# A recurrence and a long convolution on one core: a fourth spectrum buffer, a fourth input pair, fewer and larger evictions, and a new hand-written order

## The chip, the cores and the metric

One core of a Trainium2 chip runs the whole kernel in one launch. The metric is the device time of that launch in microseconds; the median of three runs is given, and lower is better.

## The reference

Two layers follow one another, for 4 batches, 6272 time steps and 256 channels. The first is a gated recurrence along time, the second a gate with a circular convolution over the full sequence, done in the reference by FFT. Cut to what matters:

```python
sig = 1.0 / (1.0 + np.exp(-f_logit))
f = lower_bound + (1.0 - lower_bound) * sig
h = np.zeros((B, D))
for t in range(S):
    h = f[:, t] * h + (1.0 - f[:, t]) * x[:, t]
    a[:, t] = h                                  # a: input of the second layer

x1, x2, x3 = split(a @ w_proj, 3)                # 256 channels each
X2 = np.fft.rfft(x2, n=S, axis=1)
H = np.fft.rfft(filter_fft, n=S, axis=0)
y = x1 * np.fft.irfft(X2 * H, n=S, axis=1) * x3
out = y @ w_out
```

## The kernel before

**How the work is tiled.** The sequence length is 6272 = 128 x 49, and the transforms are done as matmuls with small tables, in two steps each. A filter transform at the start makes the spectrum H of all channels in 16 units (`NU`), which is written to device memory and read back, unit by unit, in every batch.

**The start (`prepare`).** 13 groups of the filter, four of the 49 rows each and the last of one row, are loaded (line 610) into raw buffers that later serve other tiles. Each group is cast into one of two staging buffers `afs` (kind `fr`, line 616; the instruction carries a helper's line, 281 on ACT, 286 on DVE, 293 on POOL), rotated by matmuls in fp32r (`rot`, line 621) and evicted from PSUM in two halves, one into each of the tiles `f2` (kind `f2`, line 625). When all are there, the first filter transform (`FF1`, line 646) and the second (`FF2`, line 664) run over the 16 units, with evictions `afs` and `hw` between them, and pairs of units are stored to device memory (`hst`, line 673). `warm` (line 591) are matmuls on an identity whose result nobody reads; they are put where PE would be idle.

**The recurrence (`hgrn`).** For each batch there are 13 chunks of 512 steps. A chunk's `f_logit` and `x` are loaded (line 321) into one of three input pairs (`NX`), ACT takes the sigmoid in place (`sig`, line 324), POOL multiplies (`u`, line 326), PE transposes (`su`, line 338), `f` is made from PSUM on ACT (line 351) or DVE (line 353), and DVE scans (`scan`, line 359). The front part of the result is also copied behind its end (`wrap`, line 369), so that columns with a stride can be read past it.

**The convolution (`spectrum`).** P (`phase_p`, line 705) projects x2 in groups of four rows with eviction `x2`; F1 (line 718) and F2 (line 777) are the two steps of the transform, with eviction `A` between; then products with the spectrum: on DVE straight from PSUM (kind `prod` as "MUL", line 798), or by a copy and a product on POOL (`pm`, line 807). `mini` (line 734) and `zm` (line 740) do the same for the columns that need another treatment, and `slot` (line 782) adds these in. I2 (line 817) is the first step back, evicted to `Th`. The spectrum of a unit lies in one of three buffers `Hu` (`NH`), loaded by SP (line 755); batches run through the units in turns forwards and backwards, so that the last three units of a batch needn't be loaded for the next.

**Gate and output.** `gate` projects x1 and x3 (`x13`, line 387), evicts them (`xs`) into two tiles `x1s` and `x3s`, and multiplies to `zt` (`z`, line 417, or directly on DVE, line 408). `phase_o` has, for 13 groups of rows, the last step back (`I1`, line 851), the product with z (`y`, line 857), the output projection (`proj`, line 869), an eviction (`o`) to one of three output tiles `osb` (`NO`) and a store (line 879).

**What sets the order.** Every step is recorded as an operation with what it reads and writes. The string `ORDER` (line 123) then lists all operations in the order in which they are given out, each with its engine and its PSUM bank. So the order on each engine is written out; nothing is moved at run time, and each engine works through its own list, waiting on semaphores. All loads, stores, spectrum loads and some wraps go through SP's one list. Operations of several stages and of two batches stand between one another: the recurrence of the next batch, for one, runs inside the convolution of this one. PSUM has eight banks, and most matmul operations take two.

Of the kernel before, what the change touches and what calls it, by code (L numbers as in the profile page):

```python
# [9 lines left out]
F32 = mybir.dt.float32  # L10
# [11 lines left out]
S = 6272  # L22
# [10 lines left out]
NH = 3  # L33
NO = 3
WARM = 24
# [4 lines left out]
FS = 1.0 / 8.0  # L40
HS = 64.0 / S / FS
# [4 lines left out]
NX2 = 13  # L46
# [13 lines left out]
class Plan:  # L60
# [63 lines left out]
    "A0gA1AA5gA6AA+gBDgBIgBNgBSgAAYAOYABIACIAPIApQAdQAzYAqQAoQAkQAyQARIA2QA/YA4AA3AAQAAVYAXYBXgAhSAlSBhgBAQBJYBCAAUIA"  # L124
    "WIAfSBBIA7SBEAAvUBcgBFUBOYBGEBHEAiWBKWBTYBLGBrgBMGBPUBREBYYAnWASABmgA9CA8KBwgBZWBiIBUQBdYBbOBVIBQEBjSBsYBlCBaGAT"
    "IBeUBgEBfEBnIBtWEFgAYYBuGBkCBWIBoUBxIAZYAaYBqEByQBzAB0AAxSD5gBpMB3SB4KD7AB5QB6IB7YBvOB+UD6gCASCBKB8QB/EB9AD8YCJU"
    "ADgAEYCKMCHSCDQCICCEICCYEHACQUCLYD9SERgETAEGgEBWD+KD/KEIYCREECGEDOCOQCPACMUCNEESgEUYCTQAFgCUAEJSEKKELKCXUCSYCYEE"
    "NQEdgB1YB2YEegEOAEVUAHAEfAEPIEgYEWMEXMEZWCeSCfCEpgEYYCZQCgSEaGEbOCaACcQCdICbYEqgCnUChCCiYE1gE2gEhSElWFBgCoMErAEs"
    "YAKAEiCFCgEjKEkYEmGEnOCpQCqACwUCrYAIACjQCxME3AE4YCkAEtSAJAEuKEvKExWFLgCuUGHgEyGEzOCvECyYCsQFMgFDAFEYE5UE6ME7ME9S"
    "CtAE+CFVgE/KEwYC5WE8YC6GCzQC0AC+WFNAFFUFIQFWgFfgFggFGMC2gC/GFJIDASC3WFOYDBCFHMC4GC7YDCYFXAFYYDHSC8WFKIFPUFQMFSQF"  # L130
    "pgFqgFRMC9GDICDDWDJSFTAFUIFZUFaMDEGDKCDLYFbMDOWFhAFiYFcQFzgF0gDPGFdAFeIDQSDRCDSYDZWDMUDTSFjQDNMCGgFrAFsYAGgDaGDU"
    "CFkIFlICmgDeWDfGDXUDYEDbYF1AF2YALADgSDhKFmWF9gF+gFnOFoODcUDdEFtQFuAFvIDpSCFgFwUDnWDqCDjSFxEFyMAMAE0YDiYEEYEcYEoY"
    "DoGDrYF/AGAYF3QF4IDkCFAYDuWDvOANAMegF5IDwUDxEC1gF6SF7CF8KEAYDsWEMYJbUJcVJeNMqgDyYJgQJhRGBSDtGClgJdECVgEQYJfYJiAG"
    "CKDzWJjBJkYGDKDWgGEUD3QGIgJlSJmTGFMGGMD0GD2gGtgJnKJorGJUGKED4ADVgGPWGQOGbSGcCGdUGeMGLQGMAGRSGSKGVUGWMMgAGXQGYIGZ"
    "SGaCDFgGTWGUOCWgMsAGNUGOMGhQGiIDGgGfSGgCJqWJrXD1gJvUJxMJwQJyoJzYJsGJtHJuYGjSGkCJ0RGpUGqEJ1QJ2BJ3IJ4YGuSGwqGxYGlW"
# [58 lines left out]
def kernel(  # L194
# [753 lines left out]
```

## Time and profile before

| what | value |
|---|---|
| median of three runs | 462.13 us (459.31 to 463.2) |
| span of the profiled execution | 460.2 us (its own time isn't given beside it; the median is 1.9 us longer than this span) |
| busy PE, DVE, ACT, POOL | 96%, 90%, 88%, 67% |
| mean granted clock of TensorE | 0.996 |
| moved by DMA | 121.40 MB, mean 264 GB/s |

An engine's busy time is the time in which at least one of its instructions ran. Matmuls are pipelined and their ends are modelled, so PE shown as busy is not PE at its peak. The chain of work is followed back from the last instruction, at each step to what released it. A row of a group gives line, engine, operation, tiles, shapes and count, then the busy time and the mean nanoseconds of one, then the idle time just before them and what ended it. A row of the stretches gives the stretch, its length, busy time and count of each engine, the granted clock, the share of DMA and GB/s.

### The profile page before, as it was taken

The numbers are of one execution on the slowest core, as the hardware profiler recorded it, in microseconds if no ns is written. First come the engines' busy times: TensorE is split into PE (matmuls) and PEld (weight loads), VectorE is DVE, ScalarE is ACT, GpSimd is POOL, SyncE is SP. The second block draws the span as 40 slices with busy tenths as digits, with TensorE's granted clock in tenths as the row PEclk, the third lists the DMA queues.
The fourth block names the chain that finished last, engine by engine and source line by source line (L and its number), as shares of the span: only waits on it lengthen the run. The fifth ranks groups of instructions, "written<-read, shape, count | busy, mean of one in ns | idle before, by whom it ended". The sixth has DMA issues, their size and how long they took to land.

```text
span 460.2 us, 14622 instructions
## 1 busy us (share of the span) xinstructions
PE 439.7 (96%) x6009; PEld 344.3 (75%) x6009; DVE 412.1 (90%) x471; ACT 402.7 (88%) x582; POOL 310.2 (67%) x293
## 2 busy tenths in 40 slices
PE   7799989999989999999999999999999999999997
PEld 5677778766756889778667889767768897777786
DVE  8689998899999996998999996999999987999872
ACT  6799988799999997899999988999998868989663
POOL 6889766188999643778898435789996603857400
PEclk9899999999999999999999999999999999999999
DMA  8967898986997997386887996579869830756176
GB/s 333 390 268 288 315 307 283 349 284 219 309 353 250 358 315 276 139 246 218 307 300 280 318 317 239 214 248 318 255 235 315 306 138 13 230 200 205 57 287 275
DMA packets 44242, 121.40 MB, mean 264 GB/s; under 512 B 4240, under 2 KB 6672, under 8 KB 44176
## 3 DMA queue, kind: packets, MB, share of 16 engines
q1 hardware_dynamic: 44176, 120.47, 74.0%
q8 instruction: 47, 0.77, 0.7%
q14 instruction: 19, 0.16, 0.1%
HBM read 87.69 MB, written 31.98 MB: 260 GB/s over the span
## 4 chain that ended last, share of the span: by engine, by line
PE 63%; DVE 12%; ACT 11%; DMA 5%; issue 5%; POOL 2%; SPq 0%; DVEq 0%; ACTq 0%; POOLq 0%
PE PS L387 14%; PE PS L817 8%; PE PS L869 7%; PE PS L338 7%; PE PS L705 6%; PE PS L777 6%; PE PS L718 5%; DVE HA L359 5%; PE PS L851 4%; DMA FL<-in_f_logit_dram 3%; DVE ys L857 2%; DVE X L286 2%; ACT FL L324 2%; PE PS L646 2%; ACT fTs L351 1%
## 5 line engine op out<-in xcount | busy, mean ns | idle before, releaser
L326 POOL TENSOR_TENSOR XT<-XT,FL 128x1024 f32<-128x1024 f32 (+1 forms) x52 | 116.9, 2251 | 50.3 <-ACT FL L324 41.9
L359 DVE TENSOR_TENSOR_SCAN HA<-fTs,HA,PS 128x512 f16<-128x512 f32 (+1 forms) x96 | 112.5, 1200 | 2.8 <-ACT fTs L351 1.7
L798 DVE TENSOR_TENSOR PP<-PS,Hu 98x1008 f16<-98x1008 f32 x87 | 101.3, 1197 | 3.4 <-ACT HA L281 1.4
L387 PE MATMUL PS<-HA,W 128*128 128x490 f16 (+1 forms) x416 | 100.4, 367 | 0.9 <-DVE X L286 0.4
L807 POOL TENSOR_TENSOR PP<-HA,Hu 98x1008 f16<-98x1008 f16 x41 | 86.2, 2107 | 1.7 <-PE PS L817 1.0
L281 ACT CAST HA<-PS 128x1024 f16<-128x1024 f32 (+1 forms) x94 | 77.0, 849 | 5.1 <-PE PS L718 3.4
L417 POOL TENSOR_TENSOR zt<-x1s,x3s 128x490 f16<-128x490 f32 (+1 forms) x43 | 52.3, 1222 | 41.8 <-ACT x3s L281 22.9
L857 DVE TENSOR_TENSOR ys<-PS,zt 128x1024 fp32r<-128x1024 f32 (+1 forms) x52 | 58.5, 1149 | 9.5 <-PE PS L851 5.0
L283 ACT ACTIVATE osb<-PS 128x1024 f32<-128x1024 f32 (+1 forms) x51 | 49.9, 992 | 13.9 <-PE PS L869 11.2
L351 ACT ACTIVATE fTs<-PS,nomc 128x512 f32<-128x512 f32 (+1 forms) x89 | 58.3, 679 | 3.7 <-PE PS L338 2.3
L387 PEld LDWEIGHTS <-W 128*128 128x128 f16 x416 | 35.4, 97 | 31.7 <-issue 5.4
L869 PE MATMUL PS<-Wo,ys 128*128 128x256 f32 x392 | 57.7, 292 | 1.3 <-DVE ys L857 1.1
L283 ACT ACTIVATE x1s<-PS 128x490 f32<-128x490 f32 (+1 forms) x92 | 53.5, 594 | 5.0 <-PE PS L387 3.0
L817 PEld LDWEIGHTS <-PP 98*128 98x128 f16 x1024 | 48.7, 98 | 10.6 <-issue 3.1
L324 ACT ACTIVATE FL<-FL 128x1024 f32<-128x1024 f32 (+1 forms) x52 | 53.0, 1026 | 2.2 <-DMA FL<-in_f_logit_dram 2.1
L869 PEld LDWEIGHTS PS<-Wo,ys 128*128 128x128 f32 x392 | 49.4, 188 | 5.8 <-DVE ys L857 2.2
L817 PE MATMUL PS<-VA,PP 98*128 98x98 f16 x512 | 52.2, 207 | 1.5 <-ACT x1s L283 0.8
L817 PE MATMUL PS<-VB,PP 98*128 98x98 f16 x512 | 51.9, 207 | 0.0
L281 ACT CAST Th<-PS 128x784 f16<-128x784 f32 x58 | 48.2, 830 | 2.6 <-PE PS L817 1.6
L338 PE MATMUL PS<-iden,FL 64*128 64x64 f32 x784 | 44.8, 230 | 1.6 <-DVE HA L359 0.9
L705 PE MATMUL PS<-W,HA 128*128 128x256 f16 x392 | 44.4, 273 | 1.0 <-ACT X L281 1.0
L705 PEld LDWEIGHTS <-HA 128*128 128x128 f16 x392 | 42.9, 142 | 1.9 <-issue 1.3
(113 smaller groups left out, 724.3 us busy)
## 6 DMA issues: line engine op xcount, KB each, us to landing
Hu<-H SPq DMA_DIRECT2D x55, 512.0 KB, 4.4
FL<-in_f_logit_dram SPq DMA_DIRECT2D x48, 512.0 KB, 5.4
XT<-in_x_dram SPq DMA_DIRECT2D x48, 512.0 KB, 5.5
out_dram<-osb SPq DMA_DIRECT2D x48, 512.0 KB, 4.3
X<-in_moe_filter_fft_dram SPq DMA_DIRECT2D x9, 512.0 KB, 7.1
H<-Hu SPq DMA_DIRECT2D x4, 512.0 KB, 6.2
Hu<-in_moe_filter_fft_dram SPq DMA_DIRECT2D x2, 512.0 KB, 9.8
H<-Hu SPq DMA_DIRECT2D x4, 256.0 KB, 6.5
```

What stands on the lines that cost most here:

```text
L281: nc.scalar.copy(dst, src)
L283: nc.scalar.activation(dst, src, AF.Copy, scale=scale)
L326: op("u", {"POOL": 0.1 + 0.553 * nb}, lambda e, xt=xt, ft=ft: nc.gpsimd.tensor_tensor(xt, xt, ft, op=AOP.mult), r=[("ft", k)], w=[("xt", k)])
L338: nc.tensor.transpose(bank(pb)[:, at[p] + j:at[p] + hn:nb], src[ps, j, cols], iden[ps, ps])
L359: nc.vector.tensor_tensor_scan(h, fT, bank(pb)[:, 512 - hn:512 + hn], init, op0=AOP.mult, op1=AOP.add),
L387: nc.tensor.matmul(PS[:, p, 0:n], W13[:, kh, js], HA[:, HB[kh] + t0:HB[kh] + t0 + n], start=(kh == 0), stop=(kh == 1))
L705: nc.tensor.matmul(pp[:, r - r0, :], column(HB[kh], q_of(r)), W2[:, kh, :], start=(kh == 0), stop=(kh == 1))
L798: nc.vector.tensor_tensor(pr, px.unsqueeze(1).broadcast_to([TB, 2, UE, 63]), hh, op=AOP.mult)
L807: nc.gpsimd.tensor_tensor(pr, spec[:, o, :, 1:64].unsqueeze(1).broadcast_to([TB, 2, UE, 63]), hh, op=AOP.mult)
L817: nc.tensor.matmul(PS[:, ib + o, pr * TB:(pr + 1) * TB], PP[:TB, k, o, n, 2 * pr:2 * pr + 2, :], v[:TB], start=(n == 0), stop=(n == 1))
L857: nc.vector.tensor_tensor(late["ys"][:, yk, :, 0:rn * 128], PS[:, cb:cb + 2, 0:rn * 128], late["zt"][:].rearrange("p k r m -> p k (r m)") ...
L869: nc.tensor.matmul(po[:, i, :], late["ys"][:, yk, kh, i * 128:(i + 1) * 128], Wo[:, kh, :], start=(kh == 0), stop=(kh == 1))
```

## The change

- The spectrum gets a fourth buffer, `Hx`, whose space is also one of the two `afs` tiles of the start. A batch then keeps four units for the next.
- In batch 0 every fourth chunk is loaded into a new tile `gx`, a fourth input pair. `gx` takes the place of `x1s` and `x3s`, whose evictions therefore wait for the transposes of the last chunk that used it (tag `sx`).
- The even filter groups up to 10 (`PLAIN`) are rotated in float32 straight from the raw buffer; the other seven are cast and rotated in fp32r as before. The two tiles `f2` become one, and each group has one eviction of 1024 elements a partition. The space of `zt` is then free only when all first filter transforms are done.
- P has 12 groups instead of 13; the last has five rows and takes three banks.
- The product `zm` is one instruction for two.
- Outputs are evicted into two tiles of their own, or into lent ones: the two product buffers and two halves of the tile A, by the lists `LENT` and `LAST`.
- Tables that were two tiles are one; W2 is converted by two instructions instead of four; the channel order in W2 and Th is another.
- `WARM` is 36 operations of two matmuls instead of 24 of four. `ORDER` is new throughout: other engines for some evictions, 18 wraps on SP instead of 6, and other places for nearly every operation.

```diff
-NH = 3
-NO = 3
-WARM = 24
+NH = 4
+NO = 2
+WARM = 36
+PLAIN = (0, 2, 4, 6, 8, 10)
-NX2 = 13
+NX2 = 12
+LENT = (2, 3, 4, 5, 2, 3, 0, 1, 0, 1, 0, 1, 0)
+LAST = (2, 3, 4, 5, 0, 1, 2, 3, 4, 5, 0, 1, 2)
...
+    gx = konst.tile([128, 2048], F32, name="gx")
...
-    Hu = konst.tile([128, NH, 2, 2, UE * 64], F16, name="Hu")
+    Hu = konst.tile([128, NH - 1, 2, 2, UE * 64], F16, name="Hu")
+    Hx = konst.tile([128, 2, UE, 64], F32R, name="Hx")
...
-            k = count["x"] % NX
-            count["x"] += 1
-            xt, ft = XT[:, k, 0:nb], FL[:, k, 0:nb]
+            k = c % (NX + 1) if b == 0 else count["x"] % NX
+            count["x"] += b > 0
+            if k < NX:
+                xt, ft = XT[:, k, 0:nb], FL[:, k, 0:nb]
+            else:
+                xt, ft = (gx[:, at:at + 1024].rearrange("p (j d) -> p j d", d=D)[:, 0:nb] for at in (0, 1024))
...
-                op("xs", either(n), x1_out, w=[("x1s", j, 0)], src=x13[0])
+                op("xs", either(n), x1_out, r=["sx"], w=[("x1s", j, 0)], src=x13[0])
...
-        f2 = [pool_.tile([128, NEP // 2 * PF + 16], F32R, name=f"f2{p}")
-              for p, pool_ in enumerate((head, tmp))]
+        f2 = head.tile([128, NEP * PF + 16], F32R, name="f2")
...
-        afs = tmp.tile([128, 2, 2, UE, 64], F32R, name="afs")
+        afs = [tmp.tile([128, 2, UE, 64], F32R, name="afs"),
+               Hx]
...
+            if g in PLAIN:
+                fr, ft, turner = raw, et, rot[:].bitcast(F32)
+            else:
+                j = g // 2 % 2
+                fr, ft, turner = afs[j].rearrange("m r i k -> m (r i k)").rearrange(
+                    "m (r d) -> m r d", d=D), [("af", j, 0), ("af", j, 1)], rot
+                op("fr", ...)
...
-            for p in range(2):
-                op("f2", either(128 * rn), lambda e, pb, r0=r0, rn=rn, p=p: copy(
-                    e, both(fv[p][:, :, r0:r0 + rn]), ...
+            op("f2", either(256 * rn), lambda e, pb, r0=r0, rn=rn: copy(
+                e, both(fv[:, :, r0:r0 + rn]), ...
...
-        for g, r0 in enumerate(range(0, Q, 4)):
-            rn = min(4, Q - r0)
+        for g in range(NX2):
+            r0 = 4 * g
+            rn = Q - r0 if g == NX2 - 1 else 4
+            nb = (rn + 1) // 2
...
-            for e2 in range(2):
-                nc.vector.tensor_tensor(
-                    zp[:TB, q % 2, e2],
-                    PS[:TB, pb + e2, 0:2 * n].rearrange("p (k i) -> p k i", k=2)
-                    .unsqueeze(1).broadcast_to([TB, 2, 2, n]),
-                    Hm[:TB, e2, :, :, es], op=AOP.mult)
+            px = PS[:TB, pb:pb + 2, 0:2 * n]
+            px = bass.AP(tensor=px.tensor, offset=px.offset,
+                         ap=[px.ap[0], px.ap[1], [0, 2], [n, 2], [1, n]])
+            nc.vector.tensor_tensor(zp[:TB, q % 2], px, Hm[:TB, :, :, :, es], op=AOP.mult)
...
-            k = count["o"] % NO
-            count["o"] += 1
+            k = (LENT if b < B - 1 else LAST)[g]
+            if k < NO:
+                tags = [("osb", k)]
+            elif k < NO + NP:
+                tags = [(t, k - NO, o) for o in range(2) for t in ("P", "Pz")]
+            else:
+                tags = [t for i in range(2) for t in At(2 * (k - NO - NP) + i) + Ax(2 * (k - NO - NP) + i)]
...
-        op("pre", {"SP": 0.01}, turn_head, r=FF1[:NU], w=["cz"])
+        op("pre", {"SP": 0.01}, turn_head, r=FF1, w=["cz"])
```

More of the change, by code (lines that the diff above doesn't have):

```diff
@@ L40 @@
 FS = 1.0 / 8.0
+HP = 128
+HT = 64
 HS = 64.0 / S / FS
@@ L624, in prepare @@
[L624 to L629 removed]
+            rt = op("rot", {"PE": (0.43 if g in PLAIN else 0.12) * rn}, rotate, r=ft + ["rot"], take=2)
@@ L648, in prepare @@
                 f1 = op("FF1", {"PE": 0.475}, first,
-                        r=[("f2", g, u // 8) for g in range(13)] + ["D1r", "f2e"],
+                        r=[("f2", g) for g in range(13)] + ["D1r", "f2e"],
                         w=[("FF1", u, h)], take=2)
```

253 lines of the change are left out of this document (129 added, 124 removed).

## The prediction

> **What bounds the kernel now.** I read the page first (busy shares, the chain of work), then the busy time by stage, then what each stage waits for.
>
> ```profile
> span 460.2 us, 14622 instructions
> PE 439.7 (96%) x6009; PEld 344.3 (75%) x6009; DVE 412.1 (90%) x471; ACT 402.7 (88%) x582; POOL 310.2 (67%) x293
> PE 63%; DVE 12%; ACT 11%; DMA 5%; issue 5%; POOL 2%; SPq 0%; DVEq 0%; ACTq 0%; POOLq 0%
> ```
>
> No engine is idle for long: PE, DVE and ACT all work around nine tenths of the span, and the chain lies on PE for 63% of it. So an average tells little, and I cut the span at the places where the work changes: the first filter transform (23.7), the first P matmul of each batch (75.5, 172.7, 273.0, 371.4) and the last I2 (431.3).
>
> ```profile
> core 0: us, PE busy (x) PEld busy (x) DVE busy (x) ACT busy (x) POOL busy (x), PEclk, DMA share, GB/s
> 0.00:23.70 23.70, 17.85 (x101) 13.40 (x101) 18.14 (x49) 17.22 (x27) 18.34 (x37) 0.93 0.94 363
> 23.70:75.50 51.80, 48.55 (x604) 37.26 (x605) 48.42 (x54) 49.05 (x73) 43.28 (x50) 1.00 0.82 292
> 75.50:172.70 97.20, 92.72 (x1368) 71.78 (x1366) 90.53 (x98) 88.32 (x128) 69.31 (x55) 1.00 0.88 303
> 172.70:273.00 100.30, 98.43 (x1443) 77.56 (x1442) 93.56 (x99) 92.60 (x135) 72.06 (x59) 1.00 0.76 268
> 273.00:371.40 98.40, 96.99 (x1426) 76.57 (x1425) 91.27 (x97) 91.50 (x135) 72.92 (x59) 1.00 0.75 261
> 371.40:431.30 59.90, 59.57 (x737) 45.64 (x735) 53.92 (x64) 49.76 (x73) 33.60 (x35) 1.00 0.43 144
> 431.30:460.20 28.90, 25.58 (x344) 22.07 (x341) 16.27 (x15) 14.30 (x15) 0.73 (x1) 1.00 0.61 242
> ```
>
> The reader is to see three kinds of stage. In the first, nothing is full but the DMA (0.94). In the second, DVE and ACT are full (48.4 and 49.1 of 51.8). In the batches PE is, with 4.5, 1.9, 1.4 and 0.3 us idle; only the tail has room again (3.3 us, and PE's figure there contains filler). Whatever the change saves on DVE and ACT can shorten a batch by no more than about PE's idle time.
>
> **The change, part by part.** *The start.* The filter (6.4 MB) sets it: at the rates below, 4 us each at 337 to 404 GB/s, 6.3 MB are in by 17.6 us. The first transform starts 6 us later.
>
> ```profile
> 1.60:5.60 4.00, 4.00 (x20) 2.82 (x19) 3.79 (x16) 1.36 (x2) 4.00 (x12) 1.00 0.92 337
> 5.60:9.60 4.00, 3.52 (x27) 2.86 (x26) 3.79 (x16) 3.63 (x6) 1.46 (x3) 1.00 1.03 423
> 9.60:13.60 4.00, 2.62 (x21) 1.98 (x19) 3.83 (x9) 3.18 (x6) 3.26 (x5) 1.00 1.03 411
> 13.60:17.60 4.00, 2.52 (x16) 1.93 (x16) 1.89 (x4) 3.33 (x7) 2.54 (x4) 1.00 1.02 404
> ...
> 4.66 1.04 ACT L281 CAST afs<-X 128x1024 fp32r<-128x1024 f32 x1 [2.64 <-DMA X<-in_moe_filter_fft_dram]
> ...
> 15.80 1.23 PE PS L621 x8
> ...
> 19.96 1.15 PE PS L621 x4
> 21.13 1.75 ACT f L281 x3
> ...
> 23.75 2.23 PE PS L646 x16
> ```
>
> Between the last bytes and 23.75 the chain alternates cast, rotation and eviction: there are two staging buffers, and each group is cast into one (1.04), rotated, and evicted in two pieces. The change rotates six of the 13 groups straight from the loaded float32 data, so 6 casts go (7 stay), and 26 evictions become 13. The last full group then needs one cast (1.04), four rotations (0.6, from 8 in 1.23) and one eviction of 1024 (as the x2 rows below, 1.05 to 1.22) after its landing: with three hand-overs of about 0.15, 17.7 + 3.3 = 21.0. I take 22.0, since ACT alone then carries nine such evictions and four casts, in order: -1.7 us against 23.7; ends -2.7 and 0. The float32 rotation itself has no row. It costs 24 matmuls at from 0.15 (1.23 / 8, the fp32r ones) to 0.29 (the slowest rotations, 9 in 2.62, below): 3.7 to 7.0 us on a PE that idles 5.9 us in this stage; I take the upper end, and PE's idle time there and the filler hide all but about 1 us, which lies before the last bytes. Without that cover it would go to the start in full.
>
> ```profile
> 19.96 2.62 PE L621 MATMUL PS<-afs,rot 128*128 128x256 f32 x9 [0.55 <-ACT f L281]
> 20.60:21.60 1.00, 1.00 (x6) 0.84 (x5) 0.54 (x2) 0.78 (x2) 1.00 (x4) 0.50 1.03 410
> ```
>
> The nine slow ones ran at a granted clock of 0.50. The Trainium skill, "TensorE: Matmul & The Clock Gate" (What's actually happening), says that the clock is halved after an idle window of some 3.4 us and given back after a busy one. By that rule, longer rotations keep PE awake, and the nine would save 9 x 0.14 = 1.3 us; the trace agrees in part only: the drop came behind a thin stretch (2.62 and 2.52 of 4 us busy), not an idle one. The sum leaves it out.
>
> *Evictions and products, all batches.* Counted in the two order strings, with these durations:
>
> ```profile
> L798 DVE TENSOR_TENSOR PP<-PS,Hu 98x1008 f16<-98x1008 f32 x87 | 101.3, 1197 | 3.4 <-ACT HA L281 1.4 <-DMA Hu<-H 1.0 <-PE PS L777 0.4
> L286 DVE CAST X<-PS 128x1024 f16<-128x1024 f32 x23 | 27.3, 1220 | 12.0 <-PE PS L705 9.7 <-ACT X L281 1.6 <-DMA H<-Hu 0.6
> L281 ACT CAST X<-PS 128x1024 f16<-128x1024 f32 x25 | 25.4, 1045 | 13.4 <-PE PS L705 13.4
> L281 ACT CAST X<-PS 128x256 f16<-128x256 f32 x2 | 2.6, 1316 | 0.0
> L740 DVE TENSOR_TENSOR zp<-PS,X 98x128 f16<-98x128 f32 x32 | 10.5, 371 | 1.5 <-PE PS L734 1.3
> L353 DVE TENSOR_SCALAR fTs<-PS,nomc 128x512 f32<-128x512 f32 x13 | 9.5, 738 | 0.3 <-PE PS L338 0.3
> L351 ACT ACTIVATE fTs<-PS,nomc 128x512 f32<-128x512 f32 x83 | 56.2, 701 | 1.9 <-PE PS L338 1.3
> L281 ACT CAST HA<-PS 98x512 f16<-98x512 f32 x39 | 22.0, 603 | 1.1 <-PE PS L777 0.9
> ```
>
> A one-row x2 eviction costs more (1.3) than a four-row one (1.05); the change folds it into a five-row one. That has no row: between 1.31 (1.25 x 1.045) and 2.36 (the two added). I take 1.7, nearer to the sum by elements. All four are on ACT. DVE's x2 go from 25 to 18: about -8.6; ACT's from 27 to 30: 25 x 1.045 + 2 x 1.316 = 28.8 becomes 26 x 1.045 + 4 x 1.7 = 34.0: +5.2. The zp product becomes one instruction for two: 32 x 0.371 = 11.9 becomes 16 at 0.37 to 0.74, taken 0.5: -3.9 on DVE. Three direct products leave DVE (3 x 1.197 = -3.6), and ACT gets four copies of that half instead (4 x 0.603 = +2.4). Five f evictions and eight x1/x3 evictions move from ACT to DVE; at the f durations for both, their tiles being nearly as large (490 for 512), that is 13 x 0.738 = +9.6 on DVE and 13 x 0.701 = -9.1 on ACT. Twelve wraps move to SP from POOL (9) and ACT (3). Together DVE loses about 6.5 us and ACT 1.5, wraps not counted, over four batches. Much of that can't reach the end: the X rows show x2 evictions waiting for PE, 9.7 and 13.4 us, so what a shorter x2 gives goes into that wait, and F1 is late by PE as before. Merged constant tiles, the new channel order in W2 and Th and the two fewer weight conversions change no chain here and are taken as nothing; the full ACT of the front stage would show the last as up to a microsecond of gain.
>
> *Loads.* Spectrum loads fall from 55 to 52; batch 0 gets a fourth input pair; and the order issues loads much earlier. Adding up the TensorE work that the order string has between a spectrum load and its first user, the median was 2.7, 4.1, 6.4 and 6.6 us in batches 0 to 3, with zeros in batches 0 and 1; it becomes 9.0, 8.0, 8.8 and 7.9, never below 5.5. For input loads of batch 0 it goes from 3.5 to 7.8.
>
> ```profile
> Hu<-H SPq DMA_DIRECT2D x55, 512.0 KB, 4.4
> FL<-in_f_logit_dram SPq DMA_DIRECT2D x48, 512.0 KB, 5.4
> ...
> out_dram<-osb SPq DMA_DIRECT2D x48, 512.0 KB, 4.3
> ...
> 54.92 5.97 DMA FL<-in_f_logit_dram
> 100.43 6.23 DMA Hu<-H
> 125.69 6.87 DMA FL<-in_f_logit_dram
> ```
>
> Landings take 4.4 and 5.4, so the old leads were short just in batches 0 and 1, where the chain runs through three loads; the new ones cover them. In the front stage (23.7 to 75.5) DVE's idle time is 3.4 us (51.8 less 48.4); DVE has one x1/x3 eviction there where it had three, and one f less. I take -1.8 (ends -3.4 and 0). For the three batch stages I take two fifths of PE's idle time: -1.8, -0.8, -0.6 (ends -4.5, -1.9, -1.4, and 0), the rest staying with the in-order hand-overs; for 371.4 to 431.3 nothing. Against it: F1 needs all x2, so a five-row eviction at 2.36 that ends last delays it by up to 1.1 a batch (2.36 less 1.22), 4.4 in all; four x13 matmul pairs are queued between P and F1 as cover.
>
> New waits: x1 and x3 share the fourth input pair's space, so their evictions wait for chunk 11's transposes, and z waits for all first filter transforms. Behind them on ACT and DVE stand the x2 evictions, which P and F1 need. In both orders the first x1/x3 matmul stands behind those transposes on PE anyway, which hides it; uncovered, the banks of that pair would be held until chunk 11 is transposed.
>
> *The tail, and lent buffers.* Three output buffers become six (two own, four lent from products and spectra). A lent one must be stored before the next batch writes it: the order has at least 12.9 us of TensorE work in between, against a landing of 4.3. The two own ones get 4.8 at the least, which just covers it.
>
> ```profile
> 446.50 1.02 ACT L283 ACTIVATE osb<-PS 128x1024 f32<-128x1024 f32 x1 [1.67 <-DMA out_dram<-osb]
> 454.89 0.42 DVE L857 TENSOR_TENSOR ys<-PS,zt 128x256 fp32r<-128x256 f32 x1 [2.75 <-PE PS L851]
> 453.51 1.05 PE L591 MATMUL PS<-iden 128*128 128x256 f16 x8
> ```
>
> Evictions wait 1.67 for a store, and the last small group waits 2.75 behind filler and projections. The new order has that transform before the last two projections, and stores no longer hold ACT: -2.0 (ends -4.2 and 0).
>
> Sum: 1.7 + 1.8 + 1.8 + 0.8 + 0.6 + 2.0 = 8.7 off 460.2: 451.5. The median of the runs is 462.1, 1.9 above the span of the profile, so **453.5**.
>
> **The rivals.** *PE paces everything* (0.20). For it: 63% of the chain, and 0.3 us idle before the tail, 1.4 in the batch before that. Then DVE's and the loads' savings go into longer waits elsewhere; start 1.7 and half the tail remain: 460.2 - 2.7 + 1.9 = 459.4. Against it: DVE and ACT, not PE, fill the front stage.
>
> *The SP queue gets blocked* (0.14). SP issues in order, and wraps on it rise from 6 to 18. Each waits there for its scan, and behind it stand the next loads and stores.
>
> ```profile
> SPq L321 <- PE PS L338: 84.4, 37, 10.8
> ```
>
> The queue already waits 2.3 at a load (84.4 / 37). Twelve more such stops are 27 us; it decides where a load's lead, 4.6 to 5.3 us at its shortest in the four batches, falls under the landing of 5.4. If half of it reaches the sigmoids: 453.5 + 13.7 = 467.2, slower. Against it: a wrap's scan is usually done when the load behind it finds its buffer free.
>
> *Float32 rotations as dear as four fp32r ones* (0.14): 24 x 0.60 = 14.4, with 25 others at 0.15, is 18.2 of PE from the first landing (4.7) on, ending at 22.9; with an eviction (1.05) the transform starts at 24.0, 2.0 later than forecast: 455.5. "FP8 and Floating Point Precision" (TensorE Precision Notes) in the Trainium skill states four passes for true float32; no run here shows it yet.
>
> *All load waits go* (0.12): the ends of the front and first batch stage hold (-3.4, -4.5) with the rest as taken: 453.5 - 4.3 = 449.2.
>
> **How the numbers follow.** The forecast itself has 0.40. Faster by over 1% (4.6 us, about what a measurement tells from no change; below 457.5) holds it, the float32 and the load case: 0.66. The PE case is within: 0.20. The queue case is slower: 0.14. All lower ends together give 444.0, the upper ones 466.5; the range 446 to 463 leaves out the queue case and the case that every lower end holds.
>
> **What would show it.** Right: the first filter transform before 22.5 and the first P matmul before 73; no piece of the chain on a spectrum load; no ACT wait for a store in the tail, which takes under 27.5 from the last I2. Wrong: input or spectrum loads that land after their sigmoid or product is ready; SP waits at wraps; PE idle above 4 us in the first batch stage.

## The result, and the profile after

The time went from 462.94 to 461.27 us (medians of 17 runs each), a ratio of 0.9957 [0.9937, 0.9977]: 0.4% less, where 1.9% less was forecast. The profiled execution has a span of 459.3 us (before 460.2). From its page, the span, the busy times and the chain:

```profile
span 459.3 us, 14604 instructions
PE 444.2 (97%) x6009; PEld 346.6 (75%) x6009; DVE 402.4 (88%) x450; ACT 406.7 (89%) x563; POOL 306.0 (67%) x282
PE 66%; DVE 15%; ACT 6%; DMA 5%; issue 5%; POOL 2%; ACTq 0%; SPq 0%; DVEq 0%; POOLq 0%
```

VectorE (DVE) lost 9.7 us of busy time, 3.5 at the start and 6.2 behind it, where 6.5 was forecast. ScalarE (ACT) gained 4.0 where 1.5 less was forecast, and TensorE (PE) gained 4.5: by the rows below 3.2 at the start and 4.1 in the batch stages, less 3.2 in the tail. Gained busy time isn't gained work: where instructions of one engine overlap, busy time counts the overlap once. Added up one by one, the durations of ScalarE's instructions fell from 457.1 to 448.4 us, and those of TensorE's 6009 matmuls stayed (1491.8 and 1492.0). They overlap less than before. The busy time by stage, cut at the same events as before (the last I2 of the kernel before ends at 431.5, so its tail is 28.7):

```profile
0.00:23.70 23.70, 21.09 (x114) 16.53 (x114) 14.67 (x44) 17.43 (x18) 10.77 (x27) 1.00 0.93 355
23.70:75.20 51.50, 48.82 (x617) 38.19 (x618) 47.40 (x51) 50.28 (x73) 44.23 (x53) 1.00 0.95 342
75.20:171.50 96.30, 94.13 (x1367) 72.05 (x1365) 87.92 (x93) 90.32 (x127) 67.36 (x53) 1.00 0.82 282
171.50:272.70 101.20, 99.47 (x1444) 77.89 (x1441) 91.57 (x95) 93.42 (x133) 72.32 (x57) 1.00 0.74 252
272.70:371.70 99.00, 97.76 (x1424) 76.50 (x1424) 93.31 (x97) 90.22 (x128) 70.27 (x54) 1.00 0.79 269
371.70:432.20 60.50, 60.47 (x739) 45.81 (x738) 51.96 (x59) 50.83 (x73) 40.06 (x39) 1.00 0.46 150
432.20:459.30 27.10, 22.40 (x315) 19.64 (x312) 15.55 (x15) 14.18 (x15) 1.04 (x1) 0.99 0.65 258
```

| stage | before | after | forecast | measured |
|---|---|---|---|---|
| start, to the first filter transform | 23.7 | 23.7 | -1.7 | -0.1 |
| front, to the first P | 51.8 | 51.5 | -1.8 | -0.3 |
| first P to second | 97.1 | 96.3 | -1.8 | -0.8 |
| second to third | 100.3 | 101.2 | -0.8 | +0.9 |
| third to fourth | 98.4 | 99.0 | -0.6 | +0.6 |
| fourth P to last I2 | 60.1 | 60.5 | 0 | +0.4 |
| tail | 28.7 | 27.1 | -2.0 | -1.6 |

One execution isn't exact to a few tenths of a microsecond. In the thirteen kernels below whose start is that of the changed kernel, the first transform begins between 23.2 and 24.0 us. Of nine that touch the middle batches little, eight (e2, e6, e7, e9, e10, e14, e15, e16) have 100.3 to 100.5 us from the second P to the third, as before; e1 has 101.3. So +0.9 there is scatter and the gain is zero. Only the tail, and perhaps the front and the first batch stage, gave something; the other kernels with the same tail have 26.9 to 28.1 us there, all below the 28.7 before.

The prices that the prediction had bounded, by the groups of the trace (line, engine, operation, tiles, shapes, count, busy us, mean ns of one, idle before):

```profile
L291 ACT CAST X<-PS 128x1280 f16<-128x1280 f32 x4 | 6.3, 1578 | 1.1 <-PE PS L725 1.1
L761 DVE TENSOR_TENSOR zp<-PS,X 98x256 f16<-98x256 f32 x16 | 9.6, 601 | 0.6 <-PE PS L753 0.3
L291 ACT CAST f<-PS 128x1024 fp32r<-128x1024 f32 x9 | 10.2, 1157 | 1.6 <-PE PS L637 1.5
L291 ACT CAST X<-PS 128x1024 f16<-128x1024 f32 x26 | 25.6, 1019 | 7.3 <-PE PS L725 7.2
L296 DVE CAST X<-PS 128x1024 f16<-128x1024 f32 x18 | 21.7, 1223 | 16.7 <-PE PS L725 16.7
```

The five-row eviction (1.58, taken 1.7), the single product (0.60, taken 0.5) and the filter eviction (1.16) came near what was taken. Of the five f evictions that moved to VectorE, three were of 128 elements (0.35) and not of 512 (0.74), so the 9.6 taken for the moves was about 1.2 too much. The last row shows where most of VectorE's saving went: its x2 evictions wait 16.7 us for TensorE, before 9.7. ScalarE's wait 7.2 us, before 13.4.

### The profile page after: what moved, and what is told of

Its sections match the earlier page's. It is cut to its first block, busy times and chain, and to the rows that moved or that the text cites. A ratio compares the mean times of both kernels' runs of the same rounds, so it can differ in the third digit from the quotient of the medians.

```text
span 459.3 us, 14604 instructions
## 1 busy us (share of the span) xinstructions
PE 444.2 (97%) x6009; PEld 346.6 (75%) x6009; DVE 402.4 (88%) x450; ACT 406.7 (89%) x563; POOL 306.0 (67%) x282
## 4 chain that ended last, share of the span: by engine, by line
PE 66%; DVE 15%; ACT 6%; DMA 5%; issue 5%; POOL 2%; ACTq 0%; SPq 0%; DVEq 0%; POOLq 0%
PE PS L400 15%; PE PS L725 9%; PE PS L835 9%; PE PS L887 7%; PE PS L351 6%; DVE HA L372 6%; PE PS L795 6%; PE PS L737 6%; DVE ys L875 4%; DMA FL<-in_f_logit_dram 3%; PE PS L869 2%; PE PS L661 2%; DVE PP L816 2%; DMA X<-in_moe_filter_fft_dram 1%; ACT fTs L364 1%
## 5 line engine op out<-in xcount | busy, mean ns | idle before, releaser
L339 POOL TENSOR_TENSOR XT<-XT,FL 128x1024 f32<-128x1024 f32 (+1 forms) x49 | 109.8, 2245 | 53.6 <-ACT FL L337 36.5
L825 POOL TENSOR_TENSOR PP<-HA,Hu 98x1008 f16<-98x1008 f16 x39 | 81.8, 2106 | 6.8 <-ACT HA L291 2.7
L431 POOL TENSOR_TENSOR zt<-gx 128x490 f16<-128x490 f32 (+1 forms) x43 | 52.4, 1223 | 41.1 <-ACT gx L291 16.6
L816 DVE TENSOR_TENSOR PP<-PS,Hu 98x1008 f16<-98x1008 f32 x57 | 66.7, 1199 | 0.6 <-ACT gx L293 0.5
L364 ACT ACTIVATE fTs<-PS,cc 128x512 f32<-128x512 f32 (+1 forms) x84 | 55.3, 679 | 2.8 <-PE PS L351 2.1
L835 PE MATMUL PS<-VV,PP 98*128 98x98 f16 x1024 | 55.9, 206 | 0.3
L293 ACT ACTIVATE gx<-PS 128x490 f32<-128x490 f32 (+1 forms) x87 | 50.1, 583 | 4.5 <-PE PS L400 3.1
L291 ACT CAST Th<-PS 128x784 f16<-128x784 f32 x59 | 48.4, 820 | 4.1 <-PE PS L835 3.1
L337 ACT ACTIVATE FL<-FL 128x1024 f32<-128x1024 f32 (+1 forms) x49 | 49.4, 1010 | 1.8 <-DMA FL<-in_f_logit_dram 1.6
L351 PEld LDWEIGHTS PS<-iden,FL 64*128 64x128 f32 x736 | 31.7, 138 | 16.0 <-issue 2.6
L422 DVE TENSOR_TENSOR zt<-PS,gx 128x490 f16<-128x490 f32 (+1 forms) x61 | 38.8, 647 | 1.6 <-PE PS L400 0.9
```

Of the source, the lines that this page charges most:

```text
L291: nc.scalar.copy(dst, src)
L339: op("u", {"POOL": 0.1 + 0.553 * nb}, lambda e, xt=xt, ft=ft: nc.gpsimd.tensor_tensor(xt, xt, ft, op=AOP.mult), r=[("ft", k)], w=[("xt", k)])
L351: nc.tensor.transpose(bank(pb)[:, at[p] + j:at[p] + hn:nb], src[ps, j, cols], iden[ps, ps])
L364: nc.scalar.activation(fT, sT, AF.Identity, scale=by, bias=1.0)
L816: nc.vector.tensor_tensor(pr, px.unsqueeze(1).broadcast_to([TB, 2, UE, 63]), hh, op=AOP.mult)
L825: nc.gpsimd.tensor_tensor(pr, spec[:, o, :, 1:64].unsqueeze(1).broadcast_to([TB, 2, UE, 63]), hh, op=AOP.mult)
```

## The experiments

Every kernel is the changed one with one edit; times are medians, and a ratio is to runs of the kernel before that were made beside it. Where an edit leaves work out, its expectation says what.

### The start

**e1_om_later.** Only the order is edited: GpSimd's two instructions on the lower bound stand behind its last filter casts and a table step. In the changed kernel GpSimd waited for that load, of 1 KB, ahead of two casts. From the timeline (start, us, engine, line, operation, tiles; in brackets the idle time before and what ended it) and the DMA issues (KB each, us to landing):

```profile
13.76 0.19 POOL L465 TENSOR_SCALAR cc<-wcol 128x2 f32<-128x2 f32 x1 [3.93 <-DMA wcol<-in_lower_bound_dram]
wcol<-in_lower_bound_dram SPq DMA_DIRECT2D x1, 1.0 KB, 9.4
```

> The changed kernel, with one operation moved in POOL's list: the two small instructions on the lower bound, which wait for a 1 KB load, stand behind the casts of the filter groups instead of ahead of two of them. Theory A (POOL's wait for that load, 3.9 us, sets when the last rotations run): the first filter transform starts at 22.3 or earlier instead of 23.66, and the time falls by 1 to 2 us. Theory B (the float32 rotations and the last landing set it): it starts between 23.2 and 23.7, and the time stays within 0.5 us of 461.3.

Measured: 461.06 us, ratio 0.9986 [0.9966, 1.0006], first transform at 24.2, later than either theory had it. The wait was not what held the start.

**e2_rot_short.** The six uncast groups are rotated in one pass, as the upper halves of their bits.

```diff
-                fr, ft, turner = raw, et, rot[:].bitcast(F32)
+                fr, ft, turner = raw.bitcast(mybir.dt.bfloat16)[:, :, 1::2], et, rot[:].bitcast(mybir.dt.bfloat16)[:, 1::2]
```

The float32 rotations are the dear ones. TensorE's timeline in the changed kernel, with a float32 group of four rows (two records each) between two of fp32r:

```profile
17.25 1.89 PE L637 MATMUL PS<-Hu,rot 128*128 128x256 f32 x8
19.06 0.74 PE L637 MATMUL PS<-afs,rot 128*128 128x256 f32 x4
19.64 1.89 PE L637 MATMUL PS<-X,rot 128*128 128x256 f32 x8
```

From start to start the four float32 rows take 1.81 us and the four fp32r rows 0.58: 0.45 and 0.145 a row, and 0.47 by the busy time.

> The changed kernel, with the six uncast filter groups rotated in one pass: the upper halves of the float32 values are read as bfloat16, so the filter of these groups has less precision. Theory B (float32 rotations, 0.47 us a row, keep PE full from 17 to 23 us): the first filter transform starts at 22.4 or earlier instead of 23.66, and PE idles before it. Theory A (POOL's wait for the small load): 23.2 to 23.7. Both may hold in part; then each alone gives less than half a microsecond.

Measured: 460.68 us, ratio 0.9961 [0.9933, 0.9988], first transform at 24.1, not earlier, and outside both theories. What held it stands in this kernel's chain (start, us, what); the last row is the same cast in the timeline of the changed kernel:

```profile
11.26 9.64 DMA X<-in_moe_filter_fft_dram
20.92 1.05 ACT Hx L291
22.02 0.74 PE PS L637 x4
...
20.44 1.04 ACT L291 CAST Hx<-X 128x1024 fp32r<-128x1024 f32 x1
```

The load of the last full filter group is issued at 11.26 and lands at 20.90. Its cast and rotation follow at once, and the transform begins 3.24 us behind the landing. By the landings in the traces (20.0 to 21.0 us) that distance is 3.23 to 3.25 us in fourteen kernels: the changed one (20.42), e1 (20.97), e2 and eleven others. (e10 and e16 have no record of that landing; e14 and e15 are told below.) So cheap rotations alone didn't bring the transform forward, and the scatter of the start goes with the landing.

**e14_start_both** has both edits.

> e1_om_later and e2_rot_short together: GpSimd forms the lower-bound columns behind the filter casts, and the six uncast filter groups are rotated in one pass as the upper halves of their bits (the rest of their precision is left out). Theory S (the first filter transform waits for the slower of two: GpSimd's casts behind the 3.9 us wait, and 11.3 us of float32 rotations on TensorE, so that either repair alone shows nothing): first transform at 21 to 22.3 us, 459 us. Rival L (the last filter loads, issued at 10.5 us when their buffers come free, land at some 19 us with the queue full, and what follows them, cast, rotation, eviction and four transforms' wait, is what counts): 23.3 us or later as in both, 460.5 to 461.5 us.

Measured: 461.64 us, ratio 0.9984 [0.9955, 1.0014], and the first transform at 25.3: later than with either. Theory S fails; rival L allowed 23.3 or later. The last group lands at 21.0 here, nearly as in e1 (also 21.0, transform at 24.2), so the loads don't explain the 1.1 us between the two. The reason stands in the stretches of e14_start_both (length, then PE, PEld, DVE, ACT, POOL busy with counts, granted clock, DMA share, GB/s):

```profile
8.00:12.00 4.00, 1.11 (x9) 0.49 (x6) 3.79 (x11) 3.97 (x5) 1.64 (x2) 1.00 0.96 371
12.00:16.00 4.00, 2.38 (x16) 1.75 (x16) 1.09 (x3) 4.00 (x5) 0.86 (x2) 1.00 0.95 357
16.00:18.00 2.00, 1.17 (x8) 0.98 (x9) 0.32 (x1) 0.53 (x1) 1.91 (x5) 0.89 1.03 422
18.00:20.00 2.00, 1.50 (x7) 0.82 (x6) 0.91 (x1) 1.42 (x2) 0.00 (x0) 0.50 1.03 416
20.00:22.00 2.00, 2.00 (x10) 1.36 (x9) 1.06 (x1) 1.61 (x2) 0.00 (x0) 0.50 1.03 412
```

TensorE, with less to do, is busy 1.11 of 4 us, and from 18 us on it runs at a granted clock of 0.50. Its four fp32r rotations then take 1.22 us instead of 0.74. The kernel before had such a stretch too (0.50, as the prediction's row shows). The same in e2_rot_short (first two rows), and the changed kernel's stretch (last row):

```profile
8.00:12.00 4.00, 0.64 (x5) 0.31 (x4) 3.79 (x13) 3.99 (x5) 1.04 (x1) 1.00 0.97 372
16.00:18.00 2.00, 2.00 (x11) 1.70 (x10) 0.00 (x0) 1.15 (x1) 1.47 (x3) 0.50 1.03 420
...
8.00:12.00 4.00, 4.00 (x20) 3.32 (x18) 3.79 (x12) 3.96 (x4) 1.04 (x1) 1.00 1.01 379
```

The float32 rotations fill TensorE from 8 to 12 us, and its clock is 1.00 in every stretch of the changed kernel's start. So here dear rotations kept the clock, and cheap ones lost it. In e2 it is back at 1.00 from 20 us on, before the last group lands; in e14 it is at 0.50 until 24. The Trainium skill, "TensorE: Matmul & The Clock Gate" (What's actually happening), lets the clock fall after an idle window of some 3.4 us. The trace agrees in the value, half speed; but here the stretch ahead was thinly used, and the longest idle time in it was below 2 us.

The rows show a third thing: the DMA engines are full (0.95 or more). GpSimd's last cast in e14_start_both waited for its own filter group and not for the lower bound:

```profile
15.73 1.04 POOL L301 CAST afs<-X 128x1024 fp32r<-128x1024 f32 x1 [3.14 <-DMA X<-in_moe_filter_fft_dram]
```

**e15_last_loads** is e1_om_later with less to load:

```diff
+            ln = 1 if g in (10, 11) else rn
-                raw[:, 0:rn], ff[:, r0:r0 + rn, :]), w=et, ...
+                raw[:, 0:ln], ff[:, r0:r0 + ln, :]), w=et, ...
```

> e1_om_later with two of the last filter groups loading one row of four (left out: six rows of the filter, 0.79 MB; old rows are rotated instead). Theory L (the last filter groups land at some 20.4 to 20.9 us, behind a full queue, and the first transform follows 3 us behind): first transform at 22 to 23 us instead of 24.2, total 459 to 460 us. Rival T (TensorE's float32 rotations, back to back from 17.3 to 22.9 us in the changed kernel, set it): 24 us, 461 us.

Measured: 461.19 us, ratio 0.9984 [0.9964, 1.0003], first transform at 23.15, 1.1 before e1_om_later and just under the scatter of the unchanged start. The last group has landed at 18.2 here, and yet the transform is only 0.5 earlier than in the changed kernel: TensorE's rotations are back to back from 16.8 to 22.0 us. So two things end at nearly the same time. With cheap rotations the last load holds the start (e2), with a short last load the float32 rotations do. No run relieves both, and the median moved with neither.

### The front

**e9_front_less_act** and **e16_front_all**: the first halves the `afs` evictions; the second adds the smaller spectrum loads of e10_less_dma, below, and takes half of the second filter transform off TensorE.

```diff
-                    e, af[:, :, 4 * h:4 * h + 4],
+                    e, af[:, 0, 4 * h:4 * h + 4],
...
-                    [:, :, :, 0]), w=[("af", u % 2, h)], src=f1)
+                    [:, 0, :, 0]), w=[("af", u % 2, h)], src=f1)
...
-                for r in range(2):          # second(), e16_front_all only
+                for r in range(1):
```

> The changed kernel, with the evictions between the two filter transforms halved (the imaginary half is left out): about 5.8 us less on ACT and 2.8 on DVE between 23.7 and 75.2, nothing less on PE or the DMA. Theory E (ACT and DVE fill this stage): the first P starts 3 to 5.5 us earlier than 75.2, and the time falls by as much. Theory D (the DMA, at 0.95 there, sets it): the first P starts within 1 us of 75.2.

> The cuts of e9_front_less_act and e10_less_dma, and half of the filter's second transform on TensorE (left out: its imaginary half, 16 of 32 passes). In the front stage of the changed kernel ScalarE is busy 50.3 us of 51.5, TensorE 48.8, VectorE 47.4, and the DMA engines .95; alone the cuts bought 1.0 and 0.2 us. Theory C (they bind together): 3 to 6 us off the front, first P some 69 to 72 us, total 455 to 458. Rival F (GpSimd's in-place products, 44.2 us of 51.5, or the recurrence's fixed chain set the front): no more than 1.2 us off, first P at 74 us, 459 to 460.

Measured: e9 459.64 us, ratio 0.9949 [0.9926, 0.9972], front 50.5 instead of 51.5; e16 457.91 us, ratio 0.9879 [0.9826, 0.9932], front 49.4. The front of e9 and of e16:

```profile
24.00:74.50 50.50, 48.74 (x617) 38.03 (x618) 45.16 (x51) 46.31 (x73) 44.17 (x53) 1.00 0.95 349
23.30:72.80 49.50, 46.24 (x585) 35.74 (x586) 44.88 (x51) 46.11 (x73) 44.22 (x53) 1.00 0.90 329
```

ScalarE loses 4.0 us and the front 1.0; TensorE then loses 2.5 more, and the front another 1.1. Neither is paid in full. In e16 GpSimd is busy 44.2 of 49.5, and in the chain from 23 to 76 us VectorE's scans have the largest share:

```profile
by line: DVE HA L372 31.9%; PE PS L661 16.8%; PE PS L351 8.9%; DVE fTs L366 8.9%; issue 6.4%; PE PS L725 6.0%; PE PS L400 4.6%; ACT Hu L293 3.7%; PE PS L679 3.2%; ACT fTs L364 2.5%; ACT PP L293 1.9%; PE PS L603 1.6%; DVE f L296 1.2%; ACT gx
```

### The batches

Nine kernels change the work of one engine or of several. In short:

```diff
 # e4_less_pe: x1/x3 projections           (e17_more_pe: three passes, the second twice)
-                        for kh in range(2):
+                        for kh in range(1 + (jb == 0)):
 # e5_less_evict: ym = 64 in batches 1 and 2, na = 1 in batches 1 to 3
-                   late["ys"][:, yk, :, 0:rn * 128], PS[:, cb:cb + 2, 0:rn * 128],
+                   late["ys"][:, yk, :, 0:rn * ym], PS[:, cb:cb + 2, 0:rn * ym],
...
-            PS[:, ib:ib + 2, 0:392].rearrange("p a (g c) -> p c a g", g=4)),
+            PS[:, ib:ib + na, 0:392].rearrange("p a (g c) -> p c a g", g=4)),
 # e10_less_dma: rows of a spectrum that are loaded, and rows that are stored behind it
-HP = 128
-HT = 64
+HP = 16
+HT = 8
 # e12_less_prod: nk = 1 in batches 1 to 3, but for the first two units
-            pr = PP[:TB, k, o, :, :, 1:64]
+            pr = PP[:TB, k, o, 0:nk, :, 1:64]
 # e18_half_i2
-                    for n, v in enumerate((VA, VB)):
+                    for n, v in enumerate((VA,)):
 # e11_pe_evict = e4 + e5;  e13_all = e4 + e5 + e12;  e19_all_i2 = e13 + e18
```

> The changed kernel, with the second of the two accumulating matmuls left out in half of the x1/x3 projections: 104 matmuls of 0.21 us less on PE, 5.4 us a batch, 21.6 in all; nothing else is changed. Theory P (PE paces the batches): each batch stage is shorter by 3.5 to 5.4 us until DVE and ACT are full, and the time is 442 to 449. Theory V (evictions and products on DVE and ACT pace them): the time falls by less than 5 us, to 457 or more, and PE idles the rest.

> The changed kernel, with less work on DVE and ACT in batches 1 to 3 and the same on PE: the product with z covers half of the columns in batches 1 and 2 (about 6.6 us a batch off DVE), and the eviction to Th half of them in batches 1 to 3 (about 5 us a batch off ACT). Theory V: the time falls by 8 to 15 us, to 446 to 453. Theory P: by less than 3 us, to 458 or more, with DVE and ACT waiting longer.

> The changed kernel with spectrum loads of 16 partitions instead of 128, and second stores of the filter spectrum of 8 rows instead of 64 (products use old values elsewhere): about 23 MB less through device memory in the batches and 1.8 MB less in the front stage; the same instructions on all engines. Theory D (loads that land late set the front and the batches): the first P starts 2 us or more earlier, and the time falls by 4 us or more. Theory P (PE paces the batches, ACT the front stage): the first P starts within 1 us of 75.2 and the time stays within 1.5 us of 461.3; the four spectrum buffers then bring nothing.

> The cuts of e4_less_pe and e5_less_evict together (left out: the second half of half of the x1/x3 projections; half of each y product in batches 1 and 2; half of each Th eviction in batches 1 to 3). Alone they bought 2.5 us for 21.6 us less of TensorE and 1.1 us for some 20 us less of VectorE and 15 us less of ScalarE. Theory C (TensorE, VectorE and ScalarE are co-limiting: each is over 90% busy in the same stretches of the batches, so relief of one hands the bound to the next): together clearly more than the sum, 8 to 14 us off the changed kernel, some 448 to 453 us. Rival F (something that none of these cuts touches sets the length of the batches: GpSimd's list, SP's queue of loads, or the fixed order with its hand-overs): no more than the sum of 3.6 us, 457 to 458 us.

> In batches 1 to 3, all units but the first two multiply one of the two halves of the spectrum product only (left out: the other half, on VectorE as on GpSimd): some 9.6 us less of VectorE and some 10 us less of GpSimd a batch, 29 and 30 us in all; TensorE, ScalarE and all transfers as in the changed kernel. Theory C: VectorE is the fullest after TensorE between 22 and 62 us of a batch stage (20.45 us of 21.0, 18.56 us of 19.0), and TensorE, full there by its modelled ends, is next: 2 to 6 us off, 455 to 459 us. Rival F with GpSimd as the pacemaker: the full 10 us a batch, 430 to 440 us. Rival F with SP's queue or the fixed order: nothing, 460 to 462 us.

> e11_pe_evict and e12_less_prod together (what both leave out is left out): TensorE 21.6 us, VectorE some 49 us, ScalarE some 15 us and GpSimd some 30 us less. Theory C: more than the sum of the two, 15 to 25 us off the changed kernel, some 436 to 446 us, ScalarE and TensorE the next bound. Rival F with SP's queue or the fixed order: no more than the 3.6 us of e4 and e5, 457 to 458 us.

> In half of the x1/x3 projections the second of the two passes is done twice (so their values differ): 104 passes more, TensorE 21.6 us more, the mirror of e4_less_pe, nothing else changed. Theory P (TensorE, 98% busy in the batch stages, is the bound, the others 3 to 8% behind it): paid nearly in full, 15 to 21 us more, 476 to 482 us. Rival F (fixed hand-overs and waits with slack on TensorE): a third or less, 3 to 7 us more, 464 to 468 us.

> Half of the passes of I2 left out (the products with one of its two tables): some 0.35 us a unit, 5.6 us a batch, 22 us in all off TensorE, between 22 and 62 us of a batch stage, where it is busy 99% by the records. Theory P: until VectorE and ScalarE bind, 3 to 5% behind: 1.5 to 3 us a batch, 6 to 11 us in all, 450 to 455 us. Rival F: 0 to 3 us as in e4_less_pe, 458.5 to 461.

> e13_all and the half I2 of e18_half_i2 (what both leave out is left out): beside e13_all (451.7 us) 22 us less on TensorE, with VectorE and ScalarE at 80 and 90% there. Theory P: most of it shows, 12 to 18 us off e13_all, 434 to 440 us. Rival F: 0 to 4 us off e13_all, 448 to 452 us.

Measured, with busy times and span as differences from the profile of the changed kernel:

| kernel | median us | ratio to before | PE | DVE | ACT | POOL | span |
|---|---|---|---|---|---|---|---|
| e10_less_dma | 460.51 | 0.9967 [0.9943, 0.9991] | | | | | -0.7 |
| e4_less_pe | 458.75 | 0.9913 [0.9882, 0.9943] | -11.5 | -1.3 | -1.9 | +0.2 | -2.4 |
| e18_half_i2 | 457.66 | 0.9870 [0.9819, 0.9921] | -13.6 | -1.6 | -2.8 | -0.7 | -2.3 |
| e5_less_evict | 460.13 | 0.9947 [0.9917, 0.9978] | -1.9 | -13.4 | -13.9 | 0.0 | -0.3 |
| e12_less_prod | 461.05 | 0.9988 [0.9960, 1.0016] | -0.1 | -25.2 | -1.1 | -28.4 | -0.9 |
| e11_pe_evict | 456.09 | 0.9891 [0.9857, 0.9925] | -14.1 | -15.0 | -15.8 | -0.5 | -5.7 |
| e13_all | 451.71 | 0.9797 [0.9746, 0.9848] | -16.9 | -39.2 | -16.6 | -28.6 | -9.8 |
| e19_all_i2 | 445.97 | 0.9605 [0.9555, 0.9654] | -34.2 | -40.4 | -18.0 | -29.5 | -15.3 |
| e17_more_pe | 478.28 | 1.0307 [1.0241, 1.0373] | +17.9 | +2.5 | +3.8 | +1.0 | +17.2 |

What follows, row by row. Work added on TensorE is paid 17.2 for 17.9: TensorE has no slack to hide it. Work taken from it alone is paid 2.4 for 11.5, or 2.3 for 13.6. (e17 adds and e4 leaves out the same 104 matmuls; the busy time differs because the rest overlaps more or less.) So taking as much away does not give it back: something else is just behind. It isn't VectorE and ScalarE alone (0.3 for some 13 on each), nor VectorE and GpSimd alone (0.9 for 25 and 28), nor the transfers. It is all of them: e4 and e5 together give 5.7, where the two alone give 2.7; with e12 as well 9.8, where the three alone give 3.6. These are spans of one execution each. By the medians e4 and e5 give 2.5 and 1.1 alone and 5.2 together, a surplus no larger than the kernel before moves between groups of runs (medians of 461.98 to 463.79); e12 gives 0.2, and all three give 9.6 where the sum is 3.9, which is clear of that. e5 and e12 without e4 were not run together, so how much of it needs TensorE is not shown. Each pair of theories was drawn too sharply: e11, e13, e18 and e19 end between what the two expected. e12 alone came as its rival had it (the order or SP's queue: nothing), but e13 shows that its saving counts once the other engines have less to do. The stage from the second P to the third in e17_more_pe, e4_less_pe, e13_all and e19_all_i2:

```profile
174.70:279.90 105.20, 104.10 (x1470) 80.33 (x1467) 92.63 (x95) 94.79 (x133) 72.63 (x57) 1.00 0.71 244
170.80:270.80 100.00, 96.99 (x1416) 76.27 (x1415) 91.25 (x95) 92.87 (x133) 72.52 (x57) 1.00 0.76 255
171.10:268.00 96.90, 94.23 (x1417) 75.64 (x1415) 79.14 (x95) 87.77 (x133) 61.31 (x57) 1.00 0.77 264
170.40:265.30 94.90, 90.07 (x1290) 70.15 (x1287) 78.72 (x95) 87.45 (x133) 61.21 (x57) 1.00 0.78 270
```

With more work TensorE is busy 99% of the stage. With less it is idle for 3.0 us of 100.0 and the stage keeps its length; it becomes shorter only when the others have less too. Why one engine's relief doesn't show can be read in the changed kernel, when that stage is cut further:

```profile
171.50:182.50 11.00, 11.00 (x101) 10.76 (x98) 5.84 (x5) 9.78 (x11) 3.03 (x2) 1.00 0.93 327
182.50:193.50 11.00, 10.92 (x148) 8.88 (x147) 9.03 (x10) 10.81 (x15) 8.86 (x8) 1.00 0.29 100
193.50:214.50 21.00, 20.98 (x317) 15.74 (x316) 20.45 (x23) 19.15 (x30) 16.54 (x18) 1.00 0.76 251
214.50:233.50 19.00, 19.00 (x281) 12.86 (x281) 18.56 (x22) 18.48 (x30) 17.57 (x12) 1.00 0.72 253
```

These four make up 62 of the 101 us. TensorE is full in all of them, and each time another is nearly full beside it: ScalarE (10.81 of 11.0), then VectorE (20.45 of 21.0), then VectorE, ScalarE and GpSimd (18.56, 18.48, 17.57 of 19.0). VectorE's 5.84 in the first and 88% over the span hide this. What keeps e19_all_i2 at 94.9 us, with TensorE at 95% and the others below 93%, isn't settled; hand-overs between lists in fixed order are the candidate, and no run took these away.

### The tail, and the filler

**e7_tail3**: the last batch uses three output buffers again, its order unchanged. **e6_no_late_filler**: the ten filler operations behind the first P are left out.

```diff
-LAST = (2, 3, 4, 5, 0, 1, 2, 3, 4, 5, 0, 1, 2)
+LAST = (0, 1, 2, 0, 1, 2, 0, 1, 2, 0, 1, 2, 0)    # e7_tail3
...
-            for k in range(2):
+            for k in range(2 if i < 26 else 0):       # e6_no_late_filler, in warm()
```

> The changed kernel with three output buffers in the last batch, as before the change (two own, one lent), in the same order. Theory L (lent buffers give the tail's 1.8 us): evictions wait for stores again, the tail is 28.5 to 29.5 us from the last I2 instead of 27.1, and the time rises by 1.3 to 2.3. Theory O (the order gives it, with the last small transform placed earlier): the tail stays at 27 to 27.6.

> The changed kernel without the ten filler operations that stand behind the first P: five in the batches, five in the tail, 20 matmuls of about 0.11 us. Theory P (PE paces the batches): the five in the batches cost their 1.1 us, and the time falls by 0.5 to 1.5 us. Theory V: they stand in PE's idle time, and the time stays within 0.4 us. If the filler keeps the clock up in the tail, the granted clock falls there and the time rises.

Measured: e7 465.71 us, ratio 1.0064 [1.0041, 1.0087], tail 31.5 us, 4.4 more; e6 460.99 us, ratio 0.9967 [0.9945, 0.9989], tail 27.3: the filler costs nothing. The waits of e7's tail (engine, line, waited for: us, times, longest), of which the changed kernel has none for a store:

```profile
ACT PP L293 <- DMA out_dram<-PP: 5.7, 3, 3.6
ACT osb L293 <- DMA out_dram<-osb: 3.2, 3, 2.6
```

That is more than theory L expected (28.5 to 29.5). So in the new order the tail needs the lent buffers; with three it is even slower than the old order (28.7). What the old order would do with six, and so the share of the order, no run shows.

## Why the prediction was wrong

**The start (-1.7, came -0.1): two terms mis-sized.** The first is the landing. The prediction had the last full group in at 17.7, from the 6.3 MB that had moved by 17.6; but those rows count all that the DMA engines move, not the filter alone, and in the changed kernel the group lands at 20.4 (20.90 in e2's chain). The step behind it was right: 3.3 us taken, 3.24 measured. The second is the float32 rotation. It was bounded at 0.29 a row, from fp32r rows at half clock, and measured 0.45 to 0.47: 24 rows cost 10.9 to 11.3 us and not 7.0. That TensorE's idle time and filler would hide them failed: rotations stand back to back up to the last eviction. Either alone keeps the transform above 23 us, as e2 and e15 show. The rival for the rotations put it at 24.0 and it came at 23.66, but that is luck: with cheap rotations it came no earlier. The part on the clock, left out of the sum, held, and e14 shows that the clock can take back what cheaper rotations give. The 1 KB load, which lands 9.4 us after its issue, was missed too; by e1 it didn't matter.

**The front (-1.8, came -0.3): the wrong row was read.** The gain was taken from VectorE's idle time (3.4 us), but ScalarE had just 2.7, and its busy time rose by 1.2 (49.05 to 50.28) at the same 73 instructions. VectorE indeed fell from 48.4 to 47.4, for nothing. e9 and e16 show that ScalarE's relief isn't paid in full either.

**The batch stages (-3.2, came +0.7 in this profile): the step that failed most.** "Two fifths of PE's idle time" was a guess that the loads' waits caused that idle time. Loads had the longer leads as counted, and spectrum loads left the chain; two input loads are in it still:

```profile
51.37 8.57 DMA FL<-in_f_logit_dram
245.56 6.86 DMA FL<-in_f_logit_dram
```

But taking away most of the spectrum traffic (e10) changes nothing. The chain named the load that came last; another engine was due at nearly the same time. Nor was the idle time something to win: in the first batch stage TensorE's fell from 4.5 to 2.2 us, and the stage by 0.8. The rival "PE paces everything" described these stages: TensorE has nearly the same matmuls there (1368 and 1367, 1443 and 1444, 1426 and 1424, 737 and 739 in the rows) and 1.4, 1.0, 0.8 and 0.9 us more busy time, most of VectorE's saving went into the longer x2 wait, and e17 shows that TensorE has no room. Its sum of 459.4 was 1.9 below the median of 461.27, about the 1.7 of the start that it kept. "Everything" was too much, as e4 and e18 show.

**The tail (-2.0, came -1.6): about right, and by its mechanism.** No ScalarE wait for a store is left, the tail is under 27.5 in this profile (26.9 to 28.1 in the others), and e7 brings the wait back, with more than its time. How much of the gain is the order's is not shown.

**The other rivals.** SP was not blocked by wraps; it waited there only 4.6 us for scans, and its 93.5 us at 44 input loads are no more for each than the 84.4 at 37 before:

```profile
SPq L334 <- PE PS L351: 93.5, 44, 8.7
SPq L301 <- DVE HA L372: 4.6, 2, 4.0
```

"All load waits go" failed with the batch stages. "As dear as four fp32r ones" was near for the start alone: a float32 row costs 3.1 fp32r ones. The Trainium skill, "FP8 and Floating Point Precision" (TensorE Precision Notes), states four passes; four times 0.145 would be 0.58, and the trace has 0.45.

The time lies inside the range of 446 to 463, but close to its upper end, where nearly nothing is won: of the sum of 8.7 only the tail's term came nearly in full. (Its 451.5 and 1.9 add up to 453.4, not 453.5.)

## What to carry to other kernels

Where several engines are over 90% busy in a tuned schedule, the wait that the chain names is worth little: cut the stage into stretches, look for the second-fullest engine in each, and forecast no more than its distance to the fullest. In this kernel work added to the fullest engine was paid nearly in full, while work taken from it was paid only up to the next one. Busy time is not work: with the same matmuls TensorE showed more of it, because they overlapped less. And where loads set a stage, read when the last load lands, not how many bytes have moved by then. Extra buffers pay where an engine visibly waits for a store or a load with nothing else full, as in a tail.

## What the runs showed of the hardware

- A true float32 matmul of 128x256 cost 0.45 us against 0.145 for fp32r, 3.1 times as much.
- Cheaper TensorE work made the start later: busy 1.11 and then 2.38 of 4 us, with no idle time of 2 us, the granted clock fell to 0.50, and the first transform came at 25.3 us (e14) instead of 24.2 (e1, which differs in the rotations alone).
- A load of 1 KB took 9.4 us to land behind 512 KB loads at some 360 to 420 GB/s; a filter load of 512 KB took 9.64 (e2).
